# Subtraction of the maximum in one softmax part on GpSimd instead of VectorE

## The chip, the cores and the metric

The kernel runs on one core of one Trainium2 chip. The metric is the device time of one execution in microseconds (us). The core has five engines with instruction queues of their own: TensorE (PE in the profile; its weight loads PEld), VectorE (DVE), ScalarE (ACT), GpSimd (POOL) and SyncE (SP), which issues the transfers.

## The reference

A dynamic convolution feeds a Fourier mixing step, a normalization and an MLP, for 8 batches of 4224 rows of 192 values:

```python
w = weight_gen - np.max(weight_gen, axis=-1, keepdims=True)   # (8, 4224, 8 heads, 7 taps)
w = np.exp(w)
w = w / (np.sum(w, axis=-1, keepdims=True) + 1e-09)
# each row: 7 taps over the row and the 6 rows before it, per head of 24 columns
out = np.einsum('bshk,bskhg->bshg', w, x_unf)                 # x of the next stage

mixed = np.real(np.fft.fft(np.fft.fft(x, axis=1), axis=2))
u = x + mixed
un = (u - mean(u)) / np.sqrt(var(u) + 1e-06)                  # over the 192 columns
ch = np.maximum(un @ w_ch1, 0.0) @ w_ch2                      # 192 -> 768 -> 192
return u + ch
```

## The kernel before

A batch's 4224 rows lie as 128 partitions x 33 rows (N2 = 33). The kernel is written as generators (streams) that are interleaved by due times; the tile framework then schedules each engine's queue from the order in which the instructions are written and from its own estimate of when each is ready. So an edit in one place can change the order of instructions everywhere behind it.

For each batch:

- `softmax_taps(b, parts)` loads the tap weights (7 per head and row) and turns them into softmax weights: maximum over the 7 taps (VectorE), subtraction (VectorE), exponential in place (ScalarE), sum, addition of 1e-9, reciprocal (VectorE). For the first two batches this is done in three parts of rows: 0 to 5, 29 to 33, and the middle, 5 to 29, which has 24 rows x 8 heads = 192 maxima of 1344 weights per partition. The maxima, and later the reciprocals, lie in a tile `m`. For the first two parts of batch 0 it is a tile in SBUF (`wm_92` in the rows below: `b == 0 and lo == 0` makes it, the second part takes it over), for the middle part of batch 0 one in PSUM (`wm_110`).
- `conv(b)` multiplies the weights by the reciprocals (`wp`, `wq`, `wa`), then for each chunk of rows c and tap k the shifted rows of `x_sb` by the weights (`pr_c_k`). In batch 0, for some chunks TensorE adds the products up with an identity matrix (`pa_c`, line L446; PE_SUMS), GpSimd makes a few of the products (L439; POOL_TAPS) and ScalarE others (L409; ACT_TAPS, from `wa`); for the other chunks GpSimd adds (`u += pr`, L450). Chunk 8 is the single row 0 (`u_8`, products `pr_8_k`). The products of TensorE's chunks share three buffers. Then the rows are folded (`sm`), transformed along one axis by TensorE (`pg`), combined (`gt`, from `up`) and written to DRAM (`g_d`).
- `transform(b)` reads them back (`g`), multiplies (`pp`, L517), and ScalarE copies the result to `pq` (L521 to L531).
- `mix(b, g)` makes the second transform of row group g (`eo`, L546), and adds it to `u` (ScalarE's copy `ot`, VectorE L552 to L556).
- `norm(b, g)` normalizes (`bn`, `rs`, `un`) and splits into two float16 parts (`hl`, L609 to L612), which a transposing transfer brings to `ht`.
- `mlp(n)` is the two matrix products (`ph` L643, `hh`, `po` L666), and the result is written out.

Before the first MLP the weights, given as 64-bit floats, are converted to float32 by seven VectorE steps for each piece of 384 columns (`pa`, `t`, `pa`, `pw`, `pa`, `t`, then `pw` or `w2f`; lines L204 to L215), and split into `w1h` (ScalarE, L220) and `w1l` (VectorE, L221). The mixing of group 0 is written behind the last split of the first weight.

Of the kernel before, what the change touches and what calls it, by code (L numbers as in the profile page):

```python
# [11 lines left out]
F32 = mybir.dt.float32  # L12
# [3 lines left out]
ALU = mybir.AluOpType  # L16
AX = mybir.AxisListType
# [3 lines left out]
P = 128  # L21
N2 = 33
# [17 lines left out]
DVE_ADDS = {(1, c): 2 for c in range(2, NC)}  # L40
F32_GROUPS = 7
ACT_TAPS = {(0, 1): (0,), (0, 3): (0,), (0, 5): (0,1), (0, 7): (0,)}
TURNS = {1: 'ddpdddd', 2: 'dpddpdd', 3: 'dpddpdp'}
WARM = (20, 0, 12, 12)

# [47 lines left out]
def tile_dynconv_fnet_mlp(  # L93
# [12 lines left out]
    nc = tc.nc  # L106
    B, D = x.shape[0], x.shape[3]
    H, K = wg.shape[3], wg.shape[4]
# [7 lines left out]
    cpool = ctx.enter_context(tc.tile_pool(name="cpool", bufs=1))  # L116
# [4 lines left out]
    def pst(tag, bufs, shape, dt, name):  # L121
        return ps.tile(shape, dt, tag=tag, name=name, bufs=bufs)
# [141 lines left out]
    def softmax_taps(b, parts):  # L264

        w_sb = sb.tile([P, N2 * H, K], F32, tag="w_sb", name=f"w_{b}", bufs=2)
        if b > 0:
            m = wbanks[b][:, 4 * H * K:4 * H * K + N2 * H]
        wv = wg[b].rearrange("p r h k -> p (r h) k")
        for lo, hi in parts:  # L270
            sl = slice(lo * H, hi * H)
            if b == 0 and lo == 0:
                m = cpool.tile([P, N2 * H], F32, name=f"wm_{b}")
            elif b == 0 and hi < N2:
                m = pst("ph", 3, [P, 512], F32, f"wm_{b}")[:, 0:N2 * H]
            n = (hi - lo) * H
            nc.sync.dma_start(w_sb[:, sl], wv[:, sl])
            yield None
            nc.vector.tensor_reduce(out=m[:, sl], in_=w_sb[:, sl], axis=AX.X, op=ALU.max)
            nc.vector.tensor_tensor(out=w_sb[:, sl], in0=w_sb[:, sl],  # L280
                                    in1=m[:, sl].unsqueeze(2).broadcast_to([P, n, K]), op=ALU.subtract)
            nc.scalar.activation(w_sb[:, sl], w_sb[:, sl], AF.Exp)
            yield None
            nc.vector.tensor_reduce(out=m[:, sl], in_=w_sb[:, sl], axis=AX.X, op=ALU.add)
            nc.vector.tensor_scalar_add(out=m[:, sl], in0=m[:, sl], scalar1=1e-9)
            nc.vector.reciprocal(out=m[:, sl], in_=m[:, sl])
            yield w_sb, m

    taps = {}

    def tap_step(b, n):

# [5 lines left out]
    def turns(pool, turn):  # L298

        its = {"p": iter(pool), "d": (k for k in range(K) if k not in pool)}  # L300
        return [next(its[t]) for t in turn]
# [5 lines left out]
    def conv(b):  # L307

        g_d = g_ds[b % 2]
        parts = [(0, 5), (29, N2), (5, 29)] if b < 2 else [(0, N2)]  # L310
        taps[b] = dict(gen=softmax_taps(b, parts), n=0, tiles=None)
        part_iter = iter(range(len(parts)))
        pieces = iter(X_PIECES)
# [37 lines left out]
        for grp in groups:  # L351
# [42 lines left out]
            for c, R, u, wp, pa, wq, pt, at in chunks:  # L394
                act_taps = ACT_TAPS.get((b, c), ())
                if act_taps:
# [14 lines left out]
            for i in range(K):  # L411
                for c, R, u, wp, pa, wq, pt, at in chunks:
                    order = turns(pt, TURNS[len(pt)]) if pt and pa else range(K)
                    order = [k for k in order if k not in at] + list(at)
# [405 lines left out]
```

## Time and profile before

| | |
|---|---|
| median of 3 runs | 1139.4 us (1138.05 to 1140.47) |
| the profiled execution | 1140.4 us, of which 1138.5 us are the span of the trace |
| TensorE clock granted, mean | 0.99 |
| busy share of the span | PE 95%, PEld 72%, DVE 85%, ACT 71%, POOL 76% |
| HBM read and written | 61.46 MB and 39.37 MB |

The rows quoted below are of four kinds. Rows of the timeline give start (us), duration (us), engine, line, operation, output <- inputs with shapes, the count of merged instructions, and in brackets the idle time of the engine before them with what ended it. Rows by group have after the bar the busy time in us, the mean of one in ns, and the idle time before them. Rows by stretch give the window, its length, then busy time and count for PE, PEld, DVE, ACT and POOL, the granted clock, the share of the transfer engines and GB/s. Rows of waits read: who waited for whom, total in us, number of times, longest.

A busy share is an average over stages; a wait named in brackets is the one that ended last by the trace.

### The profile page before, as it was taken

What the parts mean: (1) busy time and instruction counts of PE and PEld (TensorE: products, weight loads), DVE (VectorE), ACT (ScalarE), POOL (GpSimd) and SP (SyncE); (2) the same over time, 40 slices, a digit from 0 to 9 for tenths busy, and PEclk for the clock granted to TensorE, in tenths of its full rate; (3) what the DMA queues carried; (4) which work ended last, traced back from release to release, by engine and by line L of the source; (5) the groups of instructions that cost most, each with busy time, mean ns of one, the idle gap of its engine ahead of it and who ended that gap; (6) DMA issues with size and microseconds to landing.
All of it is one profiled execution on the core that took longest, in us unless ns stands there. A gap on an engine that the chain in (4) does not pass through costs nothing.

```text
span 1138.5 us, 23781 instructions
## 1 busy us (share of the span) xinstructions
PE 1077.6 (95%) x8476; PEld 816.1 (72%) x8476; DVE 971.3 (85%) x1821; ACT 810.2 (71%) x2522; POOL 867.2 (76%) x745
## 2 busy tenths in 40 slices
PE   5985999998999999999989999999999999999998
PEld 3454677786777867777768867777777867887777
DVE  7988999989989998999988998999899996356443
ACT  4666775456975899569864898668975898579822
POOL 4979598699969998799959998699969998011200
PEclk9996999999999999999999999999999999999999
DMA  8354245514573348415742357415562234422321
GB/s 299 133 150 111 51 115 138 167 39 123 115 205 85 94 115 207 115 50 129 200 117 67 105 106 206 126 39 125 153 144 58 71 73 98 115 56 48 85 46 47
DMA packets 156504, 128.74 MB, mean 113 GB/s; under 512 B 108571, under 2 KB 133088, under 8 KB 156384
## 3 DMA queue, kind: packets, MB, share of 16 engines
q1 hardware_dynamic: 156384, 127.21, 42.1%
q8 instruction: 67, 1.10, 0.4%
q14 instruction: 53, 0.43, 0.1%
HBM read 61.46 MB, written 39.37 MB: 89 GB/s over the span
## 4 chain that ended last, share of the span: by engine, by line
PE 51%; DVE 14%; POOL 11%; ACT 8%; issue 8%; DMA 6%; SPq 1%; POOLq 0%; DVEq 0%; ACTq 0%
PE ph L643 21%; PE po L666 18%; POOL u L450 8%; PE pp L517 5%; DVE pr L441 5%; PE eo L546 2%; DMA g<-g_d 2%; DMA g_d<-gt 2%; PE pa L446 2%; PE pg L471 2%; DVE hh L654 1%; ACT junk L590 1%; DMA ht<-hl 1%; ACT junk L586 1%; ACT hh L653 1%
## 5 line engine op out<-in xcount | busy, mean ns | idle before, releaser
L450 POOL TENSOR_TENSOR u<-u,pr 128x768 f32<-128x768 f32 (+1 forms) x390 | 645.5, 1679 | 63.1 <-DVE pr L441 43.6
L666 PEld LDWEIGHTS <-hh 128*128 128x128 f16 x4248 | 365.1, 99 | 77.2 <-DVE hh L654 5.5
L666 PE MATMUL po<-w2h,hh 128*128 128x192 f16 x2832 | 416.0, 246 | 4.2 <-DVE hh L654 4.1
L643 PE MATMUL ph<-ht,w1h 128*128 128x512 f16 (+1 forms) x1296 | 394.0, 362 | 7.1 <-DMA ht<-hl 3.9
L441 DVE TENSOR_TENSOR pr<-x_sb,wp 128x768 f32<-128x768 f32 (+1 forms) x415 | 354.0, 875 | 17.5 <-POOL u L450 13.3
L666 PE MATMUL po<-w2l,hh 128*128 128x192 f16 x1416 | 345.4, 246 | 0.0
L654 DVE SCALAR_TENSOR_TENSOR hh<-ph,hh 128x512 f16<-128x512 f32 (+1 forms) x390 | 244.8, 634 | 103.2 <-ACT hh L653 101.5
L643 PE MATMUL ph<-ht,w1l 128*128 128x512 f16 (+1 forms) x864 | 309.8, 362 | 0.0
L653 ACT ACTIVATE hh<-ph 128x512 f16<-128x512 f32 (+1 forms) x390 | 213.7, 550 | 129.8 <-PE ph L643 103.6
L643 PEld LDWEIGHTS <-w1h 128*128 128x128 f16 x1296 | 125.5, 98 | 94.7 <-DMA ht<-hl 3.2
L601 ACT ACTIVATE un<-u,rs 128x192 f32<-128x192 f32 x264 | 123.7, 536 | 24.5 <-DVE rs L596 7.9
L610 POOL TENSOR_TENSOR hl<-un,hl 128x512 f16<-128x512 f32 (+1 forms) x69 | 75.6, 1096 | 70.5 <-ACT hl L609 32.4
L643 PEld LDWEIGHTS <-w1l 128*128 128x128 f16 x864 | 85.0, 98 | 52.6 <-issue 4.0
L590 ACT ACTIVATE junk<-u,rs 128x192 f16<-128x192 f32 x244 | 110.6, 453 | 3.2
L586 ACT ACTIVATE junk<-u 128x192 f16<-128x192 f32 x244 | 88.1, 361 | 21.9 <-DVE u L556 19.2
L546 PE MATMUL eo<-cs_sb,pq 97*128 97x97 f32 x544 | 84.5, 273 | 3.5 <-DVE u L556 2.9
L521 ACT COPY pq<-pp 97x204 f32<-97x204 f32 (+1 forms) x96 | 46.7, 488 | 56.9 <-PE pp L517 56.3
L546 PEld LDWEIGHTS eo<-cs_sb,pq 97*128 97x128 f32 x544 | 77.3, 191 | 10.6 <-issue 5.2
L671 DVE SCALAR_TENSOR_TENSOR u<-po,isc,u 128x384 f32<-128x384 f32 (+1 forms) x122 | 72.5, 594 | 8.5 <-PE po L666 8.3
L464 POOL TENSOR_TENSOR sm<-u 128x382 f32<-128x382 f32 x64 | 65.6, 1025 | 5.8 <-DMA g_d<-gt 2.7
L666 PE MATMUL po<-w2f,hh 128*128 128x192 f32 x336 | 62.3, 327 | 0.0
L599 POOL TENSOR_TENSOR rs<-rs 128x4 f32<-128x4 f32 (+1 forms) x61 | 12.8, 213 | 61.5 <-ACT hh L653 37.8
(110 smaller groups left out, 1316.9 us busy)
## 6 DMA issues: line engine op xcount, KB each, us to landing
out_dram<-u SPq DMA_DIRECT2D x64, 384.0 KB
x_sb<-in_x_dram SPq DMA_DIRECT2D x48, 384.0 KB
g<-g_d SPq DMA_DIRECT2D x40, 336.0 KB
x_sb<-in_x_dram SPq DMA_DIRECT2D x8, 864.0 KB
g_d<-gt SPq DMA_DIRECT2D x32, 195.0 KB
g_d<-gt SPq DMA_DIRECT2D x32, 189.0 KB
w<-in_weight_gen_dram SPq DMA_DIRECT2D x6, 924.0 KB
x_sb<-in_x_dram SPq DMA_DIRECT2D x8, 672.0 KB
```

Of the source, the lines that this page charges most:

```text
L441: last_product[b] = nc.vector.tensor_tensor(out=dst, in0=rows, in1=wk, op=ALU.mult)
L450: adder.tensor_tensor(out=u, in0=u, in1=pr, op=ALU.add)
L546: nc.tensor.matmul(eo[:, e, j, :], lhsT=pq[0:DH, e, r, r:r + P], rhs=cs_sb[:, e, :], start=True, stop=True)
L586: nc.scalar.activation(junk, uv[:, t, :], AF.Identity, accum_out=st[:, t, 0:1])
L590: nc.scalar.activation(junk, uv[:, t, :], AF.Square, bias=rs[:, 2, t:t + 1], accum_out=st[:, t, 1:2])
L601: nc.scalar.activation(halves[t // 2][:, t % 2, :], uv[:, t, :], AF.Identity, bias=rs[:, 1, t:t + 1], scale=rs[:, 0, t:t + 1])
L610: lo_eng.tensor_tensor(out=hl[:, t0:t1, 2 * P:3 * P], in0=src[:, 0:t1 - t0, 0:P], in1=hl[:, t0:t1, 0:P], op=ALU.subtract)
L643: last_ph[n] = nc.tensor.matmul(ph[:, 0:T], lhsT=wt[:, cs_], rhs=ht[:, 0:T, blk], start=(i == 0), stop=(i == len(terms) - 1))
L653: nc.scalar.activation(a[:, 0:T], ph[:, 0:T], AF.Relu)
L654: nc.vector.scalar_tensor_tensor(out=l[:, 0:T], in0=ph[:, 0:T], scalar=0.0, in1=a[:, 0:T], op0=ALU.max, op1=ALU.subtract)
L666: nc.tensor.matmul(po[t // 2][:, t % 2, :], lhsT=hx[:, t], rhs=wx[:, c2, :], start=(c2 == 0 and i == 0), stop=(c2 == NH - 1 and i == len(t ...
L671: nc.vector.scalar_tensor_tensor(out=lt, in0=po[t // 2][:, 0:t % 2 + 1], scalar=scales[0][:, 1:2] if f32 else isc, in1=lt, op0=ALU.mult, o ...
```

## The change

The middle part of batch 0's softmax, `(0, 5)`, takes its maximum into the SBUF tile `wm_92` instead of the PSUM tile `wm_110`, and the subtraction is issued on GpSimd. The sum, the addition and the reciprocal stay on VectorE and in `wm_110`.

```diff
+GP_SUB = {(0, 5)}
...
             if b == 0 and lo == 0:
-                m = cpool.tile([P, N2 * H], F32, name=f"wm_{b}")
+                m = outer["m"] = cpool.tile([P, N2 * H], F32, name=f"wm_{b}")
...
-            nc.vector.tensor_reduce(out=m[:, sl], in_=w_sb[:, sl], axis=AX.X, op=ALU.max)
-            nc.vector.tensor_tensor(out=w_sb[:, sl], in0=w_sb[:, sl],
-                                    in1=m[:, sl].unsqueeze(2).broadcast_to([P, n, K]), op=ALU.subtract)
+            mx, eng = (outer["m"], nc.gpsimd) if (b, lo) in GP_SUB else (m, nc.vector)
+            nc.vector.tensor_reduce(out=mx[:, sl], in_=w_sb[:, sl], axis=AX.X, op=ALU.max)
+            eng.tensor_tensor(out=w_sb[:, sl], in0=w_sb[:, sl],
+                              in1=mx[:, sl].unsqueeze(2).broadcast_to([P, n, K]), op=ALU.subtract)
             nc.scalar.activation(w_sb[:, sl], w_sb[:, sl], AF.Exp)
...
-    taps = {}
+    taps, outer = {}, {}
```

The lines behind the change are one or two higher in the new kernel. The scheduler orders the instructions anew, and the order of every engine differs in places up to the end. Three places follow. A row is line, operation, output <- inputs, and the shape of the output.

VectorE (DVE) at the subtraction, before:

```order
L279 TENSOR_REDUCE wm_110<-w_91 128x192
L441 TENSOR_TENSOR pr_0_2_158<-x_sb,wp_8_127 128x768
L441 TENSOR_TENSOR pr_8_4_162<-x_sb,wp_8_127 128x192
L441 TENSOR_TENSOR pr_8_5_169<-x_sb,wp_8_127 128x192
L280 TENSOR_TENSOR w_91<-w_91,wm_110 128x1344
L441 TENSOR_TENSOR pr_0_3_172<-x_sb,wp_8_127 128x768
L441 TENSOR_TENSOR pr_8_6_176<-x_sb,wp_8_127 128x192
L284 TENSOR_REDUCE wm_110<-w_91 128x192
L441 TENSOR_TENSOR pr_0_4_179<-x_sb,wp_8_127 128x768
```

and now:

```order
L281 TENSOR_REDUCE wm_92<-w_91 128x192
L443 TENSOR_TENSOR pr_0_2_158<-x_sb,wp_8_127 128x768
L443 TENSOR_TENSOR pr_8_4_162<-x_sb,wp_8_127 128x192
L443 TENSOR_TENSOR pr_8_5_169<-x_sb,wp_8_127 128x192
L286 TENSOR_REDUCE wm_110<-w_91 128x192
L443 TENSOR_TENSOR pr_0_3_172<-x_sb,wp_8_127 128x768
L443 TENSOR_TENSOR pr_8_6_176<-x_sb,wp_8_127 128x192
L443 TENSOR_TENSOR pr_0_4_179<-x_sb,wp_8_127 128x768
```

The subtraction (L280) has gone, and the sum (L284, now L286) stands ahead of `pr_0_3` and `pr_8_6` instead of behind them. The pair of `gt_8` instructions, which stood behind the reciprocal a little later, now follows six products further on. GpSimd (POOL) now has the subtraction between its additions for chunk 8 and the product `pr_0_6`:

```order
L452 TENSOR_TENSOR u_8_128<-u_8_128,pr_8_3_155 128x192
L282 TENSOR_TENSOR w_91<-w_91,wm_92 128x1344
L452 TENSOR_TENSOR u_8_128<-u_8_128,pr_8_4_162 128x192
L441 TENSOR_TENSOR pr_0_6_165<-x_sb,wq_0_132 128x768
L452 TENSOR_TENSOR u_8_128<-u_8_128,pr_8_5_169 128x192
```

ScalarE (ACT) in the first transform, where the copies to `pq` and the two `w1h` copies of the first weight share its queue, before:

```order
L531 COPY pq<-pp_0_1_724 97x12x17
L220 ACTIVATE w1h_81<-pw_w_00_915,sc_w_889 128x384
L521 COPY pq<-pp_4_0_734 97x12x17
...
L526 COPY pq<-pp_8_0_752 97x12x17
L220 ACTIVATE w1h_81<-pw_w_01_927,sc_w_889 128x384
L521 COPY pq<-pp_8_1_759 97x12x17
```

and now:

```order
L528 COPY pq<-pp_8_0_752 97x12x17
L221 ACTIVATE w1h_81<-pw_w_00_915,sc_w_889 128x384
L523 COPY pq<-pp_8_1_759 97x12x17
...
L528 COPY pq<-pp_16_0_784 97x12x17
L221 ACTIVATE w1h_81<-pw_w_01_927,sc_w_889 128x384
L523 COPY pq<-pp_16_1_791 97x12x17
```

The first copy has moved to the place of the second, and the second eight `pq` copies further back. VectorE's `w1l` steps wait for these copies, and its conversion of the second weight (`w2f`) follows them. VectorE at the mixing of group 0, before:

```order
L208 SCALAR_TENSOR_TENSOR pw_w_0_939<-pa_w_0_938,t_w_0_940 128x384
L210 TENSOR_SCALAR pa_w_0_938<-pw_w_0_939 128x384
L213 SCALAR_TENSOR_TENSOR t_w_0_940<-raw_w_415,pa_w_0_938 128x384
L215 TENSOR_TENSOR w2f<-pw_w_0_939,t_w_0_940 128x384
L204 TENSOR_SCALAR pa_w_1_948<-raw_w_418 128x384
L206 SCALAR_TENSOR_TENSOR t_w_1_950<-raw_w_418,pa_w_1_948 128x384
L552 TENSOR_TENSOR eo_0_958<-eo_0_958,ot_0_963 128x2x97
```

and now:

```order
L209 SCALAR_TENSOR_TENSOR pw_w_0_939<-pa_w_0_938,t_w_0_940 128x384
L554 TENSOR_TENSOR eo_0_958<-eo_0_958,ot_0_963 128x2x97
L211 TENSOR_SCALAR pa_w_0_938<-pw_w_0_939 128x384
L554 TENSOR_TENSOR eo_1_1015<-eo_1_1015,ot_1_1020 128x2x97
L555 TENSOR_TENSOR eo_0_958<-eo_0_958,ot_0_963 128x194
L214 SCALAR_TENSOR_TENSOR t_w_0_940<-raw_w_415,pa_w_0_938 128x384
L555 TENSOR_TENSOR eo_1_1015<-eo_1_1015,ot_1_1020 128x194
L557 TENSOR_TENSOR u_0_130<-u_0_130,eo_0_958 128x4x97
L558 TENSOR_TENSOR u_0_130<-u_0_130,eo_0_958 128x4x95
L216 TENSOR_TENSOR w2f<-pw_w_0_939,t_w_0_940 128x384
```

Five steps of the conversion that stood ahead of the first `eo` now stand behind it. Between that `eo` and the normalization factors of group 0 (`rs`, L596) stood five conversion steps, now seven; between these and group 0's `hl` (L610) none, now two; the last step of the second piece comes behind `hl`. On ScalarE the second cast of group 2's `hl` now stands ahead of the first `hh` of the MLP instead of behind it.

## The prediction

> **What bounds the kernel now.** I read the page's busy shares and slices first, then busy times by stretch, then instructions in order of time around the changed step and wherever the new order differs. Page, parts 1, 2 and 4:
>
> ```profile
> PE 1077.6 (95%) x8476; PEld 816.1 (72%) x8476; DVE 971.3 (85%) x1821; ACT 810.2 (71%) x2522; POOL 867.2 (76%) x745
> PE   5985999998999999999989999999999999999998
> DVE  7988999989989998999988998999899996356443
> PE 51%; DVE 14%; POOL 11%; ACT 8%; issue 8%; DMA 6%; SPq 1%; POOLq 0%; DVEq 0%; ACTq 0%
> ```
>
> TensorE is the bound over most of the span, but not in the first four slices (28.5 us each), where VectorE is nearly full. Busy time by stretch (length, then each engine):
>
> ```profile
> 0.00:28.50 28.50, 16.49 (x45) 9.34 (x46) 21.75 (x42) 11.75 (x42) 14.21 (x22) 1.00 0.85 299
> 28.50:57.00 28.50, 25.67 (x80) 13.80 (x79) 28.43 (x43) 18.29 (x87) 28.03 (x21) 1.00 0.39 132
> 85.00:114.00 29.00, 16.77 (x106) 13.59 (x104) 23.96 (x78) 18.65 (x46) 28.92 (x19) 0.68 0.43 111
> 114.00:171.00 57.00, 54.86 (x313) 41.37 (x313) 55.50 (x106) 43.13 (x129) 43.86 (x33) 0.99 0.33 82
> 171.00:285.00 114.00, 104.30 (x720) 83.08 (x719) 104.21 (x207) 63.79 (x184) 99.18 (x77) 1.00 0.42 117
> 285.00:1138.00 853.00, 836.76 (x7106) 638.90 (x7104) 712.41 (x1291) 637.43 (x1967) 632.89 (x560) 1.00 0.42 107
> ```
>
> After 114 us TensorE idles 2.1 + 9.7 + 16.2 = 28 us in 1024. Whatever starts the steady part later ends the kernel later, unless part of these 28 us goes away. The moved subtraction lies in the first stretch; its result is the time at which 114 us is reached.
>
> **Part 1: the softmax itself.** Before, in order of time:
>
> ```profile
> 11.76 1.93 POOL L450 TENSOR_TENSOR u<-u,pr 128x192 f32<-128x192 f32 x3
> 12.69 1.55 DVE L279 TENSOR_REDUCE wm<-w 128x192 f32<-128x1344 f32 x1
> 14.20 1.48 DVE L441 TENSOR_TENSOR pr<-x_sb,wp 128x768 f32<-128x768 f32 x3
> 15.60 1.55 DVE L280 TENSOR_TENSOR w<-w,wm 128x1344 f32<-128x1344 f32 x1
> 17.18 1.33 ACT L282 ACTIVATE w<-w 128x1344 f32<-128x1344 f32 x1 [1.65 <-DVE w L280]
> 17.65 1.22 DVE L441 TENSOR_TENSOR pr<-x_sb,wp 128x768 f32<-128x768 f32 x2 [0.50 <-PE pa L446]
> 18.79 1.55 DVE L284 TENSOR_REDUCE wm<-w 128x192 f32<-128x1344 f32 x1
> ```
>
> Between its products VectorE subtracts at 15.60, and while ScalarE takes the exponential it makes two more products; when these end, the exponential (to 18.51) is done and the sum starts without waiting. The new order takes 1.55 us of subtraction off VectorE, but puts the sum directly behind the products of 14.20, ahead of those two products, which now cover nothing. VectorE must stand still until max, GpSimd's subtraction and exponential have run one after the other.
>
> How long GpSimd takes for 1344 elements the trace does not show. Its nearest rows:
>
> ```profile
> L450 POOL TENSOR_TENSOR u<-u,pr 128x768 f32<-128x768 f32 x342 | 618.2, 1830 | 59.8 <-DVE pr L441 41.8 <-DVE u L450 13.4
> L439 POOL TENSOR_TENSOR pr<-x_sb,wq 128x768 f32<-128x768 f32 x5 | 7.5, 1500 | 3.9 <-DMA x_sb<-in_x_dram 3.2 <-POOL u L450 0.7
> L384 POOL TENSOR_TENSOR wq<-w,wm 128x64 f32<-128x64 f32 x2 | 0.8, 434 | 4.7 <-DVE wp L375 4.7
> ```
>
> Two full operands scaled by 1344/768 give 1.83 x 1.75 = 3.20 us, the upper end. A product with one operand repeated along the row, as the maximum is, gives 1.50 x 1.75 = 2.63. With the growth between the 64- and 768-element rows, (1.50 - 0.43)/704 per element, it is 1.50 + 576 x 0.00151 = 2.37, the lower end. I take 2.63: that row has the same kinds of operands.
>
> The Trainium skill, page "GPSIMD Engine Reference", section 3.1, speaks against such a move: per element GpSimd needs about 2.6 cycles where VectorE needs about one, and 4497 ns for a float32 tensor_tensor of 2048; my estimate from that is 2.95 us. The trace agrees within its rows (1.83 us for 768 is 2.4 ns an element, the page's figure 2.2). By it the sum below would be 0.32 us longer.
>
> The maximum ends at 14.24 (12.69 + 1.55). GpSimd is free then (11.76 + 1.93 = 13.69). I give each handoff the 0.03 that VectorE to ScalarE took before (17.15 to 17.18). So GpSimd runs from 14.27 to 16.90, the exponential from 16.93 to 18.26, and the sum starts at 18.29. At 17.65, before, VectorE had the subtraction behind it, and the two products and the sum ahead; now it has the same ahead of it at 18.29. That is a loss of 0.64 us (0.38 at the lower price, 1.21 at the upper): the stall, from 15.6, is longer than the 1.55 saved and the 0.50 of idle that was there. Break-even would be a GpSimd time of 1.99 us, below both scaled prices and the fitted one.
>
> The maximum now goes to SBUF instead of PSUM: I cost that at nothing; the two small maxima ahead went to SBUF already. On GpSimd the subtraction lies in idle time, but it delays what is queued behind it: one small addition (1.93/3 = 0.64) and then the tap product pr_0_6, which then starts at 17.5. TensorE adds the taps in turn, and pr_0_3, now behind VectorE's sum, ends at about 20.7 and is later still, so pr_0_6 costs nothing of its own. Nothing there gives VectorE its time back:
>
> ```profile
> 26.77 1.82 POOL L450 TENSOR_TENSOR u<-u,pr 128x768 f32<-128x768 f32 x1 [0.46 <-DVE pr L441]
> DVE wp L284 <- ACT w L282: 1.1, 1, 1.1
> DVE pr L441 <- PE pa L446: 0.9, 1, 0.9
> ```
>
> The first is GpSimd's next long piece, released by VectorE. The others are all that VectorE waits between 24 and 75 us, both after 64 us, where the next engines depend on it already. So 0.64 us reaches the first transform.
>
> **Part 2: the new order at 85 to 114 us.** The scheduler has also moved ScalarE's two w1h copies. Before:
>
> ```profile
> 85.02 0.57 ACT L220 ACTIVATE w1h<-pw_w,sc_w 128x384 f16<-128x384 f32 x1
> 89.37 0.56 ACT L220 ACTIVATE w1h<-pw_w,sc_w 128x384 f16<-128x384 f32 x1
> 89.97 0.62 DVE L221 SCALAR_TENSOR_TENSOR w1l<-pw_w,sc_w,w1h 128x384 f16<-128x384 f32 x1 [3.25 <-ACT w1h L220]
> 93.46 0.55 ACT L526 COPY pq<-pp 97x204 f32<-97x204 f32 x1
> 93.87 0.51 ACT L521 COPY pq<-pp 97x204 f32<-97x204 f32 x1
> 96.93 0.37 DVE L552 TENSOR_TENSOR eo<-eo,ot 128x194 f32<-128x194 f32 x1 [1.17 <-ACT ot L551]
> 97.20 0.55 DVE L207 TENSOR_SCALAR pa_w<-raw_w 128x384 int32<-128x384 int32 x1
> 97.67 0.36 DVE L553 TENSOR_TENSOR eo<-eo,ot 128x194 f32<-128x194 f32 x1
> 106.31 0.56 DVE L596 TENSOR_SCALAR rs<-st,rs 128x1 f32<-128x1 f32 x4
> 108.32 0.83 ACT L609 CAST hl<-un 128x384 f16<-128x384 f32 x2
> 108.82 0.42 DVE L610 TENSOR_TENSOR hl<-un,hl 128x256 f16<-128x256 f32 x1
> 114.67 0.42 PE L643 MATMUL ph<-ht,w1h 128*128 128x512 f16 x1 [0.55 <-DVE hl L612]
> ```
>
> The first copy now stands where the second stood (89.37), the second between the pq copies of 93.46 and 93.87. There it pushes the last transform copies, and with them eo and the mixing of group 0, by one ScalarE step: about 0.35 us (the two copies of 93.46 and 93.87 start 0.41 apart, and a little of that was wait). VectorE's wait of 3.25 us now comes twice, once for each copy, and five steps of the w2 conversion, which filled the time up to 96.93, fall behind it. Each takes 0.47 us (97.20 to 97.67). Between the mixing of group 0 and its normalization (106.31) stood five such steps, now seven: +0.94. From there to hl (108.82) stood none, now two: +0.94; before, VectorE came to hl just as ScalarE's cast was done, so nothing covers them. The first matmul of the steady part, at 114.67, follows hl. Part 2: 0.35 + 0.94 + 0.94 = 2.2 us. Its lower end is 0.3 (VectorE has slack in this stretch that I don't see, and only the copy is left), its upper 3 (the first hh on ScalarE, now behind one more cast of 0.83/2 = 0.4, and steps at their full 0.55 instead of 0.47: 7 x 0.08 more).
>
> **The sum.** 0.64 + 2.2 = 2.8 us. The profiled execution took 1140.4 (span 1138.5 and 1.9 around it), 1.0 over the median of 1139.4. So 1143.2 in its terms and 1142.2 in the median's, my forecast; its own range, from the ends of both parts, is 1140.9 (0.38 + 1.1, half of part 2) to 1143.6 (1.21 + 3). Less than 0.2%, 2.3 us, can hardly be told from no change here.
>
> **Rivals.** (a) Absorbed: part of the 28 us of TensorE idle after 114 us is wait for other engines, and a later start shortens it. Rows of TensorE's waits, 114 to 285 and then 285 to the end:
>
> ```profile
> PE po L666 <- DVE hh L654: 4.1, 4, 1.6
> PE pp L517 <- DMA g<-g_d: 2.5, 1, 2.5
> ...
> PE pp L517 <- DMA g<-g_d: 8.9, 5, 3.3
> ```
>
> GpSimd loses only 0.64, not 2.8, so the second batch's products are relatively earlier. Against: VectorE, 97% busy from 114 to 171, is as late as TensorE, and each g wait is a round trip within one batch, which moves along. With half absorbed it is 1139.4 + 1.4 = 1140.8. The lower end of part 2 leads here too (0.64 + 0.3: 1140.3).
>
> (b) Faster: the rearranged rest of the program (its order differs to the end) loses the waits for g, 2.5 + 8.9 = 11.4 us, by having more TensorE work queued ahead of each transform. It decides once more than 2.8 + 2.3 = 5.1 of these go; with 6 gone it is 1139.4 + 2.8 - 6 = 1136.2. Against: the work that TensorE has between a batch's last pg and its first pp is much the same in both orders.
>
> (c) Without effect: GpSimd as quick as 1.99 us and part 2 hidden. No row speaks for it; it lies within (a).
>
> **How the numbers follow.** The forecast has 0.47 (slower), (a) with (c) 0.31 (within 0.2%), (b) 0.22 (faster). The range runs from 1136.6, a little into (b), to 1145.0, both parts at their upper ends (1.21 + 3 = 4.2) and 1.4 more for one g wait that grows, since the waits of 2.5 and 8.9 make 1.9 each over six.
>
> **What would show it.** Right: GpSimd's subtraction at 14.4 of 2.4 to 3.2 us; VectorE's sum waiting for ScalarE some 2.7 us; GpSimd's first long add at 27.4; a second VectorE wait for w1h near 95; the first ph matmul at 117 to 118; TensorE idle after that still near 28 us. Wrong: the first ph matmul no later than 115.5 (part 2), or TensorE idle down by several us (a, b) with shorter waits for g.

## The result and the profile after

The changed kernel took 1148.24 us in the median of 5 runs (1144.01 to 1148.71), the kernel before, beside it, 1139.9 us (5 runs, 1138.05 to 1143.63): a ratio of 1.0063, interval 1.004 to 1.0086. In a second set it was 1147.33 us (9 runs) against 1139.8 us (32 runs), 1.0042 [1.0016, 1.0068]. The change made the kernel slower by about half a per cent, where 1142.2 us and at most 1145.0 us were forecast. The profiled execution took 1148.24 us, the median itself, of which 1146.5 are the span.

From the page of the changed kernel, busy time of the engines:

```profile
PE 1087.8 (95%) x8476; PEld 823.2 (72%) x8476; DVE 968.8 (85%) x1820; ACT 813.1 (71%) x2522; POOL 869.1 (76%) x746
```

TensorE runs the same 8476 products, but is busy for 1087.8 us instead of 1077.6. The shares of the others hardly differ. Ten microseconds more for the same work point to how fast each product went, and the stretches show the clock (the third column from the end):

```profile
0.00:28.50 28.50, 16.85 (x45) 9.44 (x46) 19.82 (x39) 11.75 (x42) 16.76 (x23) 1.00 0.87 308
114.00:171.00 57.00, 55.41 (x290) 39.37 (x289) 56.57 (x109) 39.14 (x110) 42.72 (x32) 0.90 0.38 82
171.00:285.00 114.00, 107.09 (x720) 84.93 (x719) 103.47 (x207) 68.86 (x203) 100.48 (x78) 1.00 0.42 117
285.00:1138.00 853.00, 840.30 (x7070) 641.30 (x7071) 712.40 (x1292) 641.05 (x1968) 632.43 (x561) 0.99 0.42 106
```

In the first stretch VectorE is busy 1.9 us less and GpSimd 2.6 us more: that is the moved subtraction. From 114 to 171 us the clock is 0.90 instead of 0.99, and TensorE does 290 products in that stretch instead of 313, although it is busy longer. Behind 285 us it is 36 products short, at a clock that rounds to 0.99 instead of 1.00. In the three windows from 114 to 1138 us TensorE idles 21.2 us instead of 28.1, and is behind all the same: part of what had been idle time now goes into slower products.

**The softmax**, in order of time on the three engines:

```profile
12.53 1.55 DVE L281 TENSOR_REDUCE wm<-w 128x192 f32<-128x1344 f32 x1
14.16 2.54 POOL L282 TENSOR_TENSOR w<-w,wm 128x1344 f32<-128x1344 f32 x1 [0.63 <-DVE wm L281]
16.73 1.32 ACT L284 ACTIVATE w<-w 128x1344 f32<-128x1344 f32 x1 [1.37 <-POOL w L282]
18.09 1.56 DVE L286 TENSOR_REDUCE wm<-w 128x192 f32<-128x1344 f32 x1 [2.56 <-ACT w L284]
21.81 0.45 DVE L374 TENSOR_TENSOR wp<-w,wm 128x224 f32<-128x224 f32 x1
23.99 0.95 DVE L443 TENSOR_TENSOR u<-x_sb,wp 128x768 f32<-128x768 f32 x1
26.75 3.71 POOL L452 TENSOR_TENSOR u<-u,pr 128x768 f32<-128x768 f32 x2
```

The chain runs as it was laid out: GpSimd subtracts in 2.54 us, the exponential follows, and VectorE stands still for 2.56 us before the sum.

**The stretch at 85 to 118 us.** ScalarE's copies, VectorE's steps, and TensorE up to the first MLP product:

```profile
89.97 0.57 ACT L221 ACTIVATE w1h<-pw_w,sc_w 128x384 f16<-128x384 f32 x1
94.37 0.56 ACT L221 ACTIVATE w1h<-pw_w,sc_w 128x384 f16<-128x384 f32 x1
90.58 0.62 DVE L222 SCALAR_TENSOR_TENSOR w1l<-pw_w,sc_w,w1h 128x384 f16<-128x384 f32 x1 [5.46 <-ACT w1h L221]
94.97 0.62 DVE L222 SCALAR_TENSOR_TENSOR w1l<-pw_w,sc_w,w1h 128x384 f16<-128x384 f32 x1 [2.71 <-ACT w1h L221]
97.89 0.37 DVE L554 TENSOR_TENSOR eo<-eo,ot 128x194 f32<-128x194 f32 x1
108.41 0.58 DVE L598 TENSOR_SCALAR rs<-st,rs 128x1 f32<-128x1 f32 x4
111.69 0.40 DVE L612 TENSOR_TENSOR hl<-un,hl 128x256 f16<-128x256 f32 x1
112.97 4.00 PE L496 MATMUL warm_hl<-hl 128*128 128x384 f16 x12 [9.71 <-ACT un L603]
117.87 0.61 PE L645 MATMUL ph<-ht,w1h 128*128 128x512 f16 x1 [0.91 <-DVE hl L614]
118.27 0.63 PE L645 MATMUL ph<-ht,w1l 128*128 128x512 f16 x1
```

`eo` is 1.0 us later than before, `rs` 2.1, `hl` 2.9, the first MLP product 3.2 (117.87 against 114.67). It also takes 0.61 us instead of 0.42, and the second 0.63 instead of 0.38, although the same 12 warming products, which nobody reads, ran just before it (4.00 us, as before).

**The clock** in stretches of 4 us; first before, then after:

```profile
114.00:118.00 4.00, 1.86 (x10) 0.96 (x10) 3.92 (x10) 3.84 (x8) 3.92 (x4) 0.90 0.54 100
118.00:122.00 4.00, 4.00 (x23) 2.23 (x23) 4.00 (x10) 1.60 (x4) 3.65 (x4) 1.00 0.00 0
122.00:126.00 4.00, 4.00 (x26) 2.58 (x25) 4.00 (x5) 1.92 (x4) 0.00 (x0) 1.00 0.22 42
344.00:348.00 4.00, 4.00 (x38) 3.17 (x38) 3.96 (x8) 2.68 (x7) 3.84 (x3) 1.00 0.64 167
```

```profile
114.00:118.00 4.00, 3.10 (x11) 1.22 (x10) 4.00 (x13) 3.97 (x6) 3.92 (x5) 0.50 0.80 98
118.00:122.00 4.00, 3.31 (x10) 1.52 (x9) 4.00 (x10) 2.81 (x7) 3.84 (x4) 0.50 0.53 98
122.00:126.00 4.00, 4.00 (x15) 2.24 (x15) 4.00 (x6) 0.92 (x2) 0.13 (x1) 0.56 0.00 0
344.00:348.00 4.00, 3.84 (x21) 3.67 (x22) 4.00 (x7) 1.96 (x6) 3.84 (x3) 0.50 1.09 220
728.00:732.00 4.00, 4.00 (x18) 2.60 (x18) 3.57 (x5) 2.39 (x6) 3.76 (x4) 0.50 0.85 167
```

Before, the clock opens within the first of these stretches. After, it stays at half until about 125, and falls below full again in one to three of these stretches from 344, 600 and 724 us on, each time behind a wait for `g`; before, only at 596. A measure that is used below: the clock time missing, (1 - granted clock) x 4 us summed over stretches of 4 us. It is 1.4 us from 112 to 130 and 1.7 from 130 on before, 6.8 and 8.5 after.

The waits for `g` after, from 114 to 285 us and from there on:

```profile
PE pp L519 <- DMA g<-g_d: 1.7, 1, 1.7
PE pp L519 <- DMA g<-g_d: 8.9, 4, 2.7
```

Their sum is 10.6 us against 11.4, so in sum they did not grow; they fall in part at other places.

### The profile page after: what moved, and what is told of

It is laid out like the page before. It is cut to its first block, busy times and chain, and to the rows that moved or that the text cites. A ratio compares the mean times of both kernels' runs of the same rounds, so it can differ in the third digit from the quotient of the medians.

```text
span 1146.5 us, 23787 instructions
## 1 busy us (share of the span) xinstructions
PE 1087.8 (95%) x8476; PEld 823.2 (72%) x8476; DVE 968.8 (85%) x1820; ACT 813.1 (71%) x2522; POOL 869.1 (76%) x746
## 4 chain that ended last, share of the span: by engine, by line
PE 43%; ACT 14%; DVE 8%; DMA 2%; issue 2%; POOL 1%; SPq 0%; DVEq 0%; ACTq 0%; POOLq 0%
PE ph L645 18%; PE po L668 17%; PE pp L519 4%; ACT junk L592 3%; ACT junk L588 3%; ACT hh L655 2%; ACT un L603 2%; DVE pr L443 2%; DVE hh L656 2%; PE eo L548 2%; PE pg L473 1%; DMA g<-g_d 1%; ACT hl L611 1%; DMA g_d<-gt 1%; POOL u L452 1%
## 5 line engine op out<-in xcount | busy, mean ns | idle before, releaser
L645 PE MATMUL ph<-ht,w1h 128*128 128x512 f16 (+1 forms) x1296 | 398.5, 364 | 6.4 <-DMA ht<-hl 2.5
```

Of the source, the lines that this page charges most:

```text
L645: last_ph[n] = nc.tensor.matmul(ph[:, 0:T], lhsT=wt[:, cs_], rhs=ht[:, 0:T, blk], start=(i == 0), stop=(i == len(terms) - 1))
```

## The experiments

The time of one kernel differs between its own executions: the kernel before took 1135.5 to 1148.3 us in the 119 runs that were made beside the experiments, and the time goes with the mean granted clock of each run (correlation -0.88; the 38 runs with a clock above 0.9875 took 1138.1 us in the mean, the 10 below 0.9815 1146.2). So differences of means with their standard errors stand here beside the ratios. Each set had its own runs of the kernel before (means 1141.5, 1140.1, 1141.0 and 1141.1 us, medians 1141.6, 1139.8, 1140.4 and 1140.3). The expectations name medians, and where these say something else than the means, the text gives both.

Theory 1: the loss comes from the new order, by the later first MLP product and by TensorE's clock behind its waits, and not from the moved subtraction. Its rivals: the move itself; a single stretch of the order that carries all; chance of the clock in the runs compared.

To change the order alone, a list of every engine's order was added to the kernels. It constrains only which instruction stands ahead of which in a queue, and adds no waits:

```diff
+ORDERS = {...}           # engine: numbers of its instructions in queue order
...
     run()
+    pin(tc, ORDERS)       # each instruction queued behind the one listed before it
```

"Old" and "new" are the orders of the kernel before and of the changed one, in three stretches: up to 65 us, 65 to 118 us (part 2 of the prediction), and behind 118 us. The old computation keeps the subtraction on VectorE. A difference is against the kernel before of the same set.

| run | computation | order up to 65 / to 118 / behind | median, us | difference of means, us | ratio [95%] |
|---|---|---|---|---|---|
| `move_alone` | new | old / old / old | 1141.8 | +0.6 ± 0.9 | 1.0003 [0.9985, 1.0022] |
| `part1_order` | new | new / old / old | 1142.3 | +1.3 ± 1.1 | 1.0007 [0.9981, 1.0032] |
| `part2_order` | old | old / new / old | 1145.0 | +3.9 ± 1.2 | 1.003 [1.0006, 1.0054] |
| `rest_order` | old | old / old / new | 1143.2 | +2.0 ± 0.8 | 1.0015 [0.9996, 1.0034] |
| `after_again` | new | new / new / new | 1147.3 | +5.5 ± 1.4 | 1.0042 [1.0016, 1.0068] |
| `undo_part2` | new | new / old / new | 1144.9 | +3.6 ± 0.9 | 1.0031 [1.0013, 1.0049] |

> Subtraction on GpSimd with its maximum in SBUF, and every engine's queue otherwise in the order of the kernel before (the sum behind the two products again). Theory, the order: the move itself costs nothing here. The subtraction takes 2.5 us on GpSimd, the exponential ends by 18.2, the two products start when TensorE frees their buffer at 17.6, and the sum starts at about 18.8 as before: first ph matmul at 114 to 115.2 us, time within 0.2% of before (ratio 0.998 to 1.002). Rival, the move (GpSimd is too slow, or it holds up the tap products behind it): first ph at 116 us or later, ratio 1.004 or more.

> Subtraction on GpSimd, with the new order only up to about 65 us (sum ahead of the two products, gt of row 0 later), the order of before behind it. Theory, the order: first ph matmul 0.3 to 0.7 us later than before (115.0 to 115.4), ratio 1.000 to 1.002. Rival, the start is what matters most (part 1 delays everything by its 0.64 and more by a lower granted clock): ratio 1.003 or more.

> Computation as before (subtraction on VectorE), with the new order only between about 65 and 118 us (w1h copies later on ScalarE, conversion steps behind the mixing of group 0), the order of before elsewhere. Theory, the order: first ph matmul at 116.7 to 117.3 (+2.2 to 2.6), VectorE waits twice for w1h. If TensorE's granted clock then also stays at half until 125 us as in the changed kernel, 3.4 us more. Ratio 1.002 to 1.005. Rival, absorbed: first ph late, time the same (ratio under 1.001). Rival, the rest of the order carries the loss: ratio under 1.002 here and over 1.004 in the run with the new order behind 118 us alone.

> Computation as before, the order of before up to about 118 us, the new order behind it. Theory, the order of the start: first ph as before (114.7), ratio 0.997 to 1.002. Rival, the rest: three stretches of half clock behind the transforms' waits (near 345, 600 and 727 us in the changed kernel, against one near 598 before), 1.7 to 3.4 us each, belong to the new order: they appear here too, ratio 1.003 to 1.006. Rival, chance: such stretches differ from run to run of one kernel whatever the order, so the granted clock differs by 0.005 or more between rounds of the same kernel and the times go with it.

> The changed kernel itself, unaltered, beside the kernel before on the chip of the other runs of this set. Theory 1 (the order of the instructions between 65 and 118 us and TensorE's clock behind it make the loss): the median lies 3 to 6 us above that of the kernel before, as the old computation with the new order of that stretch did (+3.4 us in the medians, +3.9 in the means), plus up to 1.6 us for the order behind 118 us; first MLP product near 117.9 us; in the profile more than 5 us of clock time missing between 112 and 130 us. Theory 2 (the first comparison's +7.3 us is what the change costs): +6 to +9 us again. Theory 3 (chance of the clock in the five executions, nothing else): within 1.5 us of the kernel before.

> The changed kernel with the subtraction on GpSimd and the new order everywhere, except that between 65 and 118 us each engine's queue has its old order. Theory 1: the first MLP product is back at 115.1 us (from 117.9), TensorE's clock missing between 112 and 130 us falls from 6.8 to 1 to 2 us, and the median lies 0 to 2.5 us above the kernel before, at least 2 us under the changed kernel. Theory 2 (the loss comes from the order behind 118 us, where the waits for the read-back meet the clock): first product at 115.1 too, yet the time stays within 1.5 us of the changed kernel's.

What follows. The move by itself costs nothing that can be told from the scatter, and neither does the order of the first 65 us; their first MLP products, at 115.16 and 115.25 us, came as expected. The order from 65 to 118 us costs 3.9 ± 1.2 us with nothing moved to GpSimd at all: the first MLP product comes at 118.40 us there, later than the 116.7 to 117.3 expected. The order behind 118 us adds some 2 us alone, with a ratio that lies inside the range of the theory that it costs little, and an interval that holds 1. Yet in its profile the clock falls to half four times (near 226, 268, 343 and 595 us), as the rival had it; and the mean clock of single runs of the kernel before lies anywhere from 0.978 to 0.991, so chance is part of every comparison here.

Added up (0.6, 0.7 for part 1's order over the move, 3.9, 2.0) the parts make 7.2 us; the whole measured 6.9 in the means of the first set and 5.5 ± 1.4 in the second (+7.5 in the medians, which theory 2 had expected; the nine runs fall into four at 1140.6 to 1143.5 and five at 1147.3 to 1150.1 us). Undoing the middle stretch brings the first product back to 114.74 us and leaves +3.6 ± 0.9 (+5.1 in the medians), more than the 0 to 2.5 expected: the order behind 118 us was priced too low there too. Against `after_again` it gains 2.4 us in the medians and 1.9 ± 1.5 in the means, so inside the changed kernel the price of the middle stretch is known less well than alone.

**Which part of the middle stretch.** ScalarE alone, and VectorE alone, in the new order:

> The kernel before, with ScalarE alone in the new order between 65 and 118 us (the two w1h copies later among the copies to pq), all other queues as before. It is read by the time from the first mixing product (eo) to the first MLP product, 19.5 us in the kernel before and 21.7 us in the changed one. My step (the copies cost 0.35 us, the rest is conversion steps on VectorE): 19.5 to 20.0 us, w1h waited for longer on VectorE, and eo up to 0.6 us later. Rival (the later copies carry the delay): 20.8 us or more.

> The kernel before, with VectorE alone in the new order between 65 and 118 us (four more conversion steps ahead of the last normalization steps of group 0), all other queues as before. My step (two conversion steps ahead of rs and two between rs and hl, 0.94 us each pair): from the first eo product to the first MLP product 21.0 to 21.8 us, against 19.5 before. Rival (the delay comes from ScalarE's copies or GpSimd's order): under 20.3 us.

TensorE's `eo` and first `ph` of `act_order`, then of `dve_order`:

```profile
95.97 2.59 PE L568 MATMUL eo<-cs_sb,pq 97*128 97x97 f32 x16
103.39 2.00 PE L568 MATMUL eo<-cs_sb,pq 97*128 97x97 f32 x8 [4.83 <-DVE u L578]
118.36 0.38 PE L665 MATMUL ph<-ht,w1h 128*128 128x512 f16 x1 [0.67 <-DMA ht<-hl]
```

```profile
95.19 2.25 PE L568 MATMUL eo<-cs_sb,pq 97*128 97x97 f32 x16
116.89 0.61 PE L665 MATMUL ph<-ht,w1h 128*128 128x512 f16 x1 [0.91 <-DVE hl L634]
```

From `eo` to `ph` it is 19.5 us before (95.18 to 114.67) and 21.7 in the changed kernel. VectorE's order alone gives 21.7 (95.19 to 116.89), the whole of the 2.2 us. ScalarE's alone gives 22.4, which my step had not expected: in VectorE's old order, all that stands behind the `w1l` steps waits for the later copies, and TensorE waits 4.83 us for `u`. The two do not add: either order alone is enough. As I read it, in the changed kernel VectorE's own new order uses that wait for conversions, and then has them in the way; no run separates the two there. Whether a delay of this kind is paid at the end was then timed:

> The kernel before with VectorE alone in the new order between 65 and 118 us, now timed: the conversion steps ahead of the normalization put the first MLP product 2.2 us later (21.7 instead of 19.5 us behind the first eo product). Theory 1 (a later start is paid in full, and the clock near it in small part): +2 to +4 us against the kernel before. Rival (a) of the prediction (the idle time of TensorE behind 114 us takes the delay up): within 1 us of it.

1144.7 us in the median (+4.4), +3.1 ± 0.8 us in the means, ratio 1.0024 [1.0001, 1.0046], first product at 117.39 us, 2.7 later than before. Rival (a), that TensorE's idle time takes the delay up, falls. But this run also has TensorE at half clock behind the first product (6.5 us of clock time missing from 112 to 130 us), so its time alone does not say what the delay costs and what the clock.

**The clock at the first product.** Without the 12 warming products, and with 30 more of them in the idle time:

```diff
-WARM = (20, 0, 12, 12)
+WARM = (20, 0, 0, 12)          # before_no_warm
```

```diff
         if warm:
+            keep_warm(("ph", 3), f"id{g}", ident32, ident32, 30)     # after_early_warm
             keep_warm(("ph", 3), f"hl{g}", hl[:, 0, 0:P], hl[:, T - 1, 0:2 * D], WARM[2])
```

> The kernel before in its old order without the 12 warming products of TensorE ahead of the first MLP product (WARM[2] = 0). It gives the price of the closed clock alone, with nothing later on the other engines. Theory 1: the first product stays at 114.7 us (or up to 0.6 us earlier, nothing being in its way) but takes 0.6 us, the clock is 0.5 until 4 to 10 us of products have run, 4 to 7 us of clock time are missing between 112 and 130 us, and the median rises by 2 to 4 us. Rival (the idle time of TensorE around 115 to 143 us absorbs it): within 1 us of the kernel before.

> The changed kernel in its own order, with 30 products of the identity with itself (128 x 128 x 128, float32, into the spare bank, read by nobody) on TensorE ahead of its 12 warming products, in the 9.7 us in which it sits idle from 103.3 to 113.0 us. They take about 0.2 to 0.4 us each, 8 to 10 us in all. Theory 1 (TensorE's half clock from 113 to 125.5 us costs part of the loss): the first product stays at 117.9 us, but takes 0.4 instead of 0.6 us, the granted clock is 0.9 or more from 114 to 120 us, the clock time missing between 112 and 130 us falls from 6.8 to under 3 us, and the median falls by 1.5 to 4 us against the changed kernel. Rival (TensorE's wait for VectorE and ScalarE there absorbs the clock): clock up, time within 1 us of the changed kernel's. Second rival (the added products collide with the 12): first product later than 118.3 us and no gain.

`before_no_warm`, its first products, then `after_early_warm`, TensorE from the added products on:

```profile
113.76 0.61 PE L665 MATMUL ph<-ht,w1h 128*128 128x512 f16 x1 [13.54 <-DVE hl L634]
114.16 0.63 PE L665 MATMUL ph<-ht,w1l 128*128 128x512 f16 x1
```

```profile
102.15 9.21 PE L518 MATMUL warm_id<-ident 128*128 128x128 f32 x60
112.07 2.11 PE L518 MATMUL warm_hl<-hl 128*128 128x384 f16 x12 [0.71 <-DVE hl L636]
117.02 0.39 PE L668 MATMUL ph<-ht,w1h 128*128 128x512 f16 x1 [2.84 <-DVE hl L636]
117.24 0.60 PE L668 MATMUL ph<-ht,w1l 128*128 128x512 f16 x1
```

(The 30 added products are float32; the row counts two for each.) Without warming, the clock is at half until 120 us (4.1 us missing from 112 to 130), and the time is 1141.1 us, +1.3 in the medians, +1.2 ± 1.0 in the means, ratio 1.0001 [0.9981, 1.0022]: between theory 1 (2 to 4 us) and its rival (within 1 us). With 30 more products the 12 ran in 2.11 instead of 4.00 us, so the clock was open; but TensorE then waited 2.84 us for `hl` on its way to `ht`, and from the second product on it was at half again (3.4 us missing instead of 6.3). The time is 1143.9 us, 3.5 less than `after_again` in the medians, but in the means +4.8 ± 0.9 against +5.5 ± 1.4: no gain that can be told. Neither run is a clean test. In the first, the first product also came 0.9 us earlier, nothing being in its way; in the second, the products of the MLP still ran at half clock.

The traces can be read more finely than the times. Behind 118 us the order is the same in all runs with the old order there, so one and the same instruction can be looked up in each. The fifth copy `hh` on ScalarE, in the kernel before, `before_no_warm`, `before_filled` (its added products come only behind 220 us) and `conversions_timed`:

```profile
122.89 0.60 ACT L649 ACTIVATE hh<-ph 128x512 f32<-128x512 f32 x1 [0.48 <-PE ph L643]
123.75 0.60 ACT L671 ACTIVATE hh<-ph 128x512 f32<-128x512 f32 x1 [0.48 <-PE ph L665]
125.09 0.60 ACT L675 ACTIVATE hh<-ph 128x512 f32<-128x512 f32 x1 [0.48 <-PE ph L669]
128.03 0.60 ACT L671 ACTIVATE hh<-ph 128x512 f32<-128x512 f32 x1 [0.48 <-PE ph L665]
```

| run | first MLP product against before, us | TensorE's clock behind it | fifth copy `hh` against before, us |
|---|---|---|---|
| `move_alone` | +0.5 | full from 116 us on | +0.4 |
| `part1_order` | +0.6 | full | +0.6 |
| `before_no_warm` | -0.9 | half to 120 us | +0.9 |
| `before_filled` | -0.2 | half to 122 us | +2.2 |
| `dve_order` | +2.2 | half to 124 us | +4.4 |
| `conversions_timed` | +2.7 | half to 125 us | +5.1 |
| `act_order` | +3.7 | half from 122 to 125 us | +5.6 |
| `part2_order` | +3.7 | half from 120 to 127 us | +6.7 |

The last column hardly changes up to 210 us (by less than 0.2 us). So a later first product is paid one to one up to there where the clock is full (`move_alone`, `part1_order`). In `before_no_warm` and `before_filled`, whose order is that of the kernel before throughout, half clock right behind the first product costs 1.8 and 2.4 us; in the four runs with a late first product the last column exceeds the first by 1.9 to 3.0. All eight runs with a late first product show such a stretch of half clock, the changed kernel among them. What part of it is left at the end of the program cannot be told from times that scatter by 3 us.

**The clock behind the waits for g.** Eight products that nobody reads, on TensorE ahead of the first product of some transforms, shorten its idle time there:

```diff
+FILL = {(1, 0, 0), (2, 0, 0), (4, 0, 0)}       # and (5, 0, 0) with the new order behind 118 us
...
+                for _ in range(8 * ((b, m0, e) in FILL)):
+                    nc.tensor.matmul(pp[0:DH, 0:3, :], lhsT=tab.rearrange("p a b -> p (a b)")[:, 0:DH], rhs=tab,
+                                     start=True, stop=True)
```

> The changed kernel in its own order, with 8 products of a table with itself (102 x 97 x 102, float32, into the PSUM tile that the first product of the transform then overwrites) on TensorE ahead of the first product of the transforms of batches 1, 2, 4 and 5, where it waits 1.7 to 3.1 us for g. They take about 1.7 us each time at the full clock. Theory 1 (the order behind 118 us costs through the clock, which falls after these waits): the stretches at half clock near 344, 600 and 726 us go, the clock time missing behind 130 us falls from 7 to 8 us to under 4 us, the median falls by 2 to 5 us against the changed kernel (1147.3 us in the last set), and first products stay at 117 to 118 us. Rival (the fillers delay the transforms as much as the clock had): clock up, time within 1 us of the changed kernel's or above it. Second rival (nothing that follows hangs on the clock, since TensorE waits later anyway, as the products without warming showed at 114 us): clock up, and time within 1.5 us of the changed kernel's.

> The changed kernel with the old order between 65 and 118 us (as in the run that undid that part, 1144.9 us median, +0.31%) and with the 8 fillers on TensorE ahead of the first product of the transforms of batches 1, 2, 4 and 5. Theory 1 (what the order behind 118 us costs, it costs through the clock after its longer waits for g): clock time missing behind 130 us falls from 6.9 to under 4 us and the median comes to within 1.5 us of the kernel before. Rival (that order costs something else, such as its order of transfers or of GpSimd's queue): clock up, median still 2.5 us or more above the kernel before.

> The subtraction on GpSimd in the old order everywhere, with the same 8 fillers ahead of the first product of the transforms of batches 1, 2 and 4, where the old order waits 1.8 to 3.4 us for g. Theory 1: clock time missing behind 130 us 1 to 3 us (3.4 and 1.7 us in the two profiles of this order without fillers, where the clock's mean over all runs lies at 0.985 to 0.986), the median 1 to 3 us below the kernel before, and fewer runs above 1143 us. Rival (fillers cost what they save): within 1 us of the kernel before.

> The kernel before, with the 8 fillers ahead of the first product of the transforms of batches 1, 2 and 4, and nothing else. Theory 1 (the clock after the waits for g is what makes the kernel's executions differ by 12 us): clock mean 0.987 or more, median 0.5 to 2.5 us under the kernel before, the runs above 1144 us (6 to 10 of 30 without fillers) all but gone. Rival (the fillers' own 1.7 us each cost what they save): within 0.5 us of the kernel before, with the same scatter.

| run | without fillers, us | with fillers, us | ratio with fillers [95%] |
|---|---|---|---|
| `undo_filled` | +3.6 ± 0.9 | +0.6 ± 0.8 | 1.0005 [0.9984, 1.0026] |
| `after_filled` | +5.5 ± 1.4 | +4.5 ± 1.0 | 1.0043 [1.0021, 1.0066] |
| `move_filled` | +0.6 ± 0.9 | -1.0 ± 1.0 | 0.999 [0.9967, 1.0013] |
| `before_filled` | 0 | -1.8 ± 0.8 | 0.9985 [0.9963, 1.0008] |

How the wait at 595 us looks in `before_filled`, with the clock of the stretch behind it, and a wait of `rest_order` with no fillers for comparison:

```profile
594.78 1.57 PE L538 MATMUL pp<-te_sb 102*97 102x102 f32 x16
596.96 0.94 PE L543 MATMUL pp<-te_sb,g 102*97 102x102 f32 x8 [0.61 <-DMA g<-g_d]
...
596.00:600.00 4.00, 3.39 (x31) 2.62 (x30) 4.00 (x6) 2.06 (x7) 3.30 (x2) 1.00 1.16 267
```

```profile
342.60 1.09 PE L539 MATMUL pp<-te_sb,g 102*97 102x102 f32 x8 [3.01 <-DMA g<-g_d]
343.48 1.57 PE L539 MATMUL pp<-to_sb,g 102*97 102x102 f32 x8
...
344.00:348.00 4.00, 4.00 (x25) 3.14 (x24) 2.37 (x5) 3.24 (x10) 3.84 (x3) 0.67 1.02 218
```

With the fillers the idle piece is 0.61 us, and the transform's products go at full clock (0.94 and 0.86 us for the first two groups); with an idle piece of 3.01 us the second group takes 1.57 us, nearly twice.

What a closed clock costs there can again be read at one and the same copy `hh` in runs with the old order behind 118 us. In the six whose clock closed behind the wait at 222 to 229 us (`part1_order`, `part2_order`, `act_order`, `dve_order`, `conversions_timed`, `before_no_warm`) the distance to the kernel before grows by 1.4 to 1.8 us between 210 and 240 us; in the three where it stayed open (`move_alone`, `move_filled`, `before_filled`) it changes by less than 0.3.

Do the new order's closings explain its price? In part. Without fillers, the five profiles with the new order behind 118 us miss 5.1 to 8.5 us of clock time behind 130 us (mean 6.8), the eight with the old order 1.7 to 5.1 (mean 3.6). With fillers it is 3.4 (`undo_filled`) and 5.1 (`after_filled`, where under 4 was expected) against 1.7 and 1.7. From `undo_part2` to `undo_filled` the loss falls by 3.0 ± 1.2 us in the means; in the medians from +5.1 to +2.3, which lies between theory 1 (within 1.5 us) and its rival (2.5 or more). But the same kind of fillers takes 1.8 ± 0.8 us off the kernel before as well. Beside `before_filled`, of the same set, `undo_filled` is still 2.4 ± 0.8 us longer, at nearly the same mean clock (0.9867 against 0.9872). So a share of that order's price goes through the clock behind its waits; how large a share was not shown.

In the old order the fillers gain 1.6 (the difference of the two rows of `move_filled`) and 1.8 us, the runs above 1143 us falling from 31 of 119 to 1 of 24; both intervals still hold 1, so no version is shown to beat the kernel before. In `after_filled` the gain is 1.0 ± 1.7 us, which settles nothing; its clock still closed behind two idle pieces of TensorE (1.87 us at 270.11 and 1.67 us at 345.96).

## Why the prediction was wrong

- **What bounds the kernel.** Right: TensorE, and a later start of the steady part ends the kernel later. `conversions_timed` shows it. The sign that was to speak against it, TensorE idle down by several us with shorter waits for `g`, did come (21.2 instead of 28.1 us), and the kernel was slower even so: slower products took that time.
- **Part 1, the chain.** Right in each link: subtraction 2.54 us (2.63 taken, 2.37 to 3.20 as bounds), wait 2.56 us (2.7). The Trainium skill, page "GPSIMD Engine Reference", section 3.1, gave 2.95 us by my estimate; here the row of products scaled by size was nearer. The 0.64 us that this should have cost did not arrive: GpSimd's first long addition started at 26.75 us, not 27.4. From the start of the maximum to `u` it is 11.46 us (12.53 to 23.99) against 11.32 before, a loss of 0.14. "Nothing there gives VectorE its time back" failed. In the kernel before the corresponding rows are

```profile
21.38 0.71 DVE L372 TENSOR_TENSOR wp<-w,wm 128x224 f32<-128x224 f32 x1
23.28 0.23 DVE L480 TENSOR_TENSOR gt<-pg,up 128x95 f32<-128x95 f32 x1
24.01 0.95 DVE L441 TENSOR_TENSOR u<-x_sb,wp 128x768 f32<-128x768 f32 x1
```

  The `wp` step took 0.45 instead of 0.71, and the `gt` pair of 23.28 had moved behind. I had noted that move among the changes of order and not counted it.
- **Part 2, the delay.** Right in size: 2.2 us for this stretch, and 2.2 measured from `eo` to the first product (21.7 less 19.5); with what lay ahead of it 3.2 us at the first product, where 2.8 were forecast. Its division was not right: VectorE's order alone gives all of the 2.2 (`dve_order`), and ScalarE's, priced at 0.35, gives 2.9 alone (`act_order`). The terms named for the upper end add up to 3.2, not 3 (2.2, 0.4 and 0.56).
- **The sum: here it failed.** It set the loss at the end equal to the loss at the first product, 2.8 us, with nothing for TensorE's clock, and let the order behind 118 us cost nothing in the forecast and 1.4 us at the upper end of the range ("one g wait that grows"). Two terms were missing. First, half clock behind the late first product: 1.9 to 3.0 us on top of the delay, read at the copy `hh`, in the four runs of the table with a late first product, and 1.8 and 2.4 us in the two whose order is that of the kernel before. Second, the order behind 118 us: 2.0 ± 0.8 us alone (`rest_order`, interval still holding 1) and 3.6 ± 0.9 with the move and part 1's order (`undo_part2`), though in the changed kernel the waits for `g` summed to less than before. Part of that price is in TensorE's clock behind the waits, 1.4 to 1.8 us for a closing; the rest stays open. The profile of before had the sign of it: one stretch, 596 to 600 us, with a clock of 0.57 behind the longest wait, 3.3 us.
- **The size of the middle stretch.** In time it costs 3.9 ± 1.2 us where the first product is 3.7 us later (`part2_order`), and 3.1 ± 0.8 where it is 2.7 later (`conversions_timed`). The times agree with the delay alone and with the delay plus some of the clock.
- **Rivals.** (a), absorbed: fell. (b), faster by shorter waits: the waits did sum to 0.8 us less, and the kernel was slower all the same.
- **The clock at 114 to 126 us**, which the trace suggests first as a cause, is a part of it: the two runs that tried it moved the time by no more than can be told, but neither tried it alone, and the traces show its price at the start.

What stays open: how the 7 to 8 us between the medians divide to better than 1 us; what makes `undo_filled` 2.4 ± 0.8 us longer than `before_filled` at nearly the same clock; how much of what half clock costs at the start is left at the end; and why a late first product came with half clock in all eight runs.

## What to carry to other kernels

An edit of one instruction in a scheduled kernel is mostly an edit of the order: here moving the subtraction cost nothing that could be told, and the order that came with it half a per cent. Time the move with the old order and the new order without the move before judging either. Where TensorE is the bound, a wait is not priced by its length alone: list its idle pieces of 1.5 us and more, and look at the granted clock of the 4 us behind each. Where times scatter more than the change is worth, look one and the same later instruction up in every trace: here it showed prices of 1.5 us that five or twelve runs could not.

## What was not expected of the hardware

In 17 profiles of these kernels TensorE has 74 idle pieces of 1.5 us or more behind 130 us. The granted clock of the 4 us behind them was below 0.95 after 7 of the 24 shorter than 2 us, 15 of the 30 from 2 to 2.5 us, and 14 of the 20 longer ones: in these traces a matter of chance that grows with the length, with no length that parts the two. In `move_alone` a wait of 1.8 us (at 344 us) closed it, and one of 3.34 us (at 595 us) did not. The Trainium skill, page "TensorE: Matmul & The Clock Gate", Part 1 (The HAM clock gate), says that the activity window of about 3.4 us runs freely, so that the number of slow products varies from run to run; the traces agree in that every stretch at half clock behind 130 us lasts 3.4 us or twice that. It would explain how a kernel with one order differs by 12 us between executions; no run here tests it. The page adds that the ramp costs under 1% of a typical span. Here the whole scatter of the kernel before is of that size (1135.5 to 1148.3 us, 1.1%), and larger than the change that was to be measured.

A warming stretch does not hold by itself either: behind 12 products of 4.00 us in all the first MLP product ran at full clock in `act_order` (0.38 us, with 0.67 us of idle time between) and at half in the changed kernel (0.61 us, with 0.91 us between). The length of that gap does not decide it: in `undo_filled` the product ran at half after 0.51 us, in `part2_order` (its 12 products took 3.82 us) at full clock after 1.09 us.
